# Means by VectorE's block transposes in two more groups, and Newton steps on GpSimd for every reciprocal root

## The chip, the cores and the metric

The kernel runs on one NeuronCore of a Trainium2 chip. The metric is the time of the device for one execution, in microseconds (us). The engines are TensorE (PE, its weight loads PEld), VectorE (DVE), ScalarE (ACT), GpSimd (POOL) and SyncE (SP), which starts nearly all of the DMAs.

## The reference

The first half is a linear attention with a norm over the 64 elements of a head; the second is a wide layer with the gate h * erf(softplus(h)). All in f32.

```
kv  = einsum('bhsd,bhse->bhde', k, v)          # b=8, h=8, s=576, d=64
out = einsum('bhsd,bhde->bhse', q, kv)
rms = sqrt(mean(out*out, axis=-1) + 1e-6)
x   = (out / rms * g_norm)                     # as 4608 rows of 512
h   = x @ w_in                                 # 512 -> 2048
g   = h * erf(softplus(h))
y   = g @ w_out                                # 2048 -> 512
```

## The kernel before

The 4608 rows are worked off in nine groups, T = 0 to 8, of 512 rows each: the first 512 of the 576 rows of each batch entry, and, as the last group, the eight remainders of 64 rows, which are collected in `x_last`. Within a group two heads together make 128 partitions, so a group has four pairs of heads p = 0 to 3, and x is held transposed, a block of 128 features (two heads) by 512 rows per pair. The mean over a head's 64 features is therefore a sum over 64 partitions.

The matrix products of the layer run over 16 units f of 128 hidden features, four units to a batch (`BATCH`). From group 1 on, h = x @ w_in is made of three fp32r products from two parts of each factor ("high" and "low" and a scaled sum, `upper`, `lower`, `product`), 12 matmuls of 128x512 for a block, into two PSUM banks n_ps and m_ps; three such pairs of banks go round (`pair_of_banks`). Group 0 uses plain f32 matmuls (L1201), and groups 0 and 1 use plain f32 for the second product (`project`, L834), with a lag of five units.

The work falls into four parts.

1. A prologue for group 0, in the order that `ORDER` writes out (`first_group`).
2. Groups 0 and 1 in the loop at L1156, a unit at a time. While group T is worked on, the attention of group T + 1 is made in pieces, which `pieces_of` (L1028) hands out to steps of the loop: for a pair, `visit` (the products with kv, into the PSUM tile `at`, and the square on ScalarE), then one step later `halve` and `keep_tail`, `mean`, in the step after that `norm` and the transpose of the next q (`turn`, L347), then `split`. Within a step the order of the code is: weights that are due (L1162: three or four VectorE instructions L281, L284, L287, L292 that join the two halves of the f64 words of w_in or w_out to f32), pieces of list 3 (L1166), parts of the weights (L1168), pieces of list 0 (L1170), more weights that are due (L1172), gates (L1082), the matmuls of h, the copy of h, softplus, pieces of list 1, the products of `project`, pieces of list 2. Each engine takes its instructions in this order. The weights are joined only during group 0.
3. The change to the third part (`held_sums`, L1110), with the last `mean`, `norm` and `split`.
4. Groups 2 to 8, in batches of four units (L1323), with all of their products in fp32r and all parts of the weights read back from DRAM. Here the attention of the next group is made for two pairs at once by `paired` (L542), at numbered places of a batch: place i + 1 after unit i, place 5 + j after the result of rows j.

In part 2 the mean is a matmul with a 128x128 matrix of 1/64 (`mean_w`); so that fp32r is exact enough, `halve` (L455) cuts the squares into two parts on VectorE (L459, L460) and `mean` (L462) makes four matmuls of 128x256 (L470, L471). The first pair of group 1 uses two plain f32 products instead (L476). The reciprocal root is then taken on ScalarE over 128x512: a logarithm (L482), an exponential of -0.5 times it (L483) and its square (L484), with two loads of activation tables around them (L114, L117), and `norm` adds one Newton step with two VectorE instructions (L490, L493) ahead of the product with `out` and `gm_col` (-0.5 g, L502).

In `paired`, VectorE transposes the squares in blocks of 32x32 (L629) and sums each block along the free axis (L630), so that 128x16 sums stand for 128x512 squares; four ScalarE copies of 32 partitions (L643) and an addition (L644) join the two blocks of a head. The root is taken on 128x32 for two pairs, also with logarithm, exponential and square (L649 to L651) and one Newton step (L658, L661), and a transpose of a broadcast (L665) spreads it back over 128x512, ahead of the product L674.

Of the kernel before, what the change touches and what calls it, by code (L numbers as in the profile page):

```python
# [39 lines left out]
FP32 = mybir.dt.float32  # L40
# [8 lines left out]
EPS = 1e-6  # L49
# [9 lines left out]
SQ = 32  # L59
BLOCKS = 16  # L60
ORDER = """
kv0 fill0 q0 fill1 q_out0 kv_out0 result0 kv1 kv_out1 q1 square0 q_out1 mean0 log0 result1 kv2 kv_out2
# [8 lines left out]
def kernel(  # L71
# [328 lines left out]
    def keep_prepared():  # L400
        kept.pop()()
        turn(1, 0)

    def attention(T, p):

        st = {}

        halves = T > 1 or (T == 1 and p > 0)
# [4 lines left out]
        two = halves_of  # L413

        bd = kv_of(T, p)

        def square_tile(name):
            return qt_tile(name)[:, 0:G]

        def visit():  # L420


            qT = ready.pop((T, p))
            at = st["at"] = at_tile()
            x = halves_of(qT[:, 0:G])
            for a, i in ((0, 0), (0, 1), (1, 0), (1, 1)):
                nc.tensor.matmul(  # L427
                    at[rows_of[i if a else 1 - i], a, 0 : 2 * P],
                    lhsT=bd[rows_of[i], a * D : (a + 1) * D],
                    rhs=x[rows_of[i], a],  # L430
                    start=True,
                    stop=True,
                )
# [11 lines left out]
            nc.scalar.activation(two(st["sq"]), st["o"], AF.Square)  # L445

# [7 lines left out]

        def halve():  # L455
            sq = st.pop("sq")
            hi = st["hi"] = attp.tile([P, G], FP32R, name="sq_hi", tag="rms_r")
            lo = st["lo"] = attp.tile([P, G], FP32R, name="sq_lo", tag="sq_lo")
            nc.vector.tensor_copy(out=hi, in_=sq)  # L459
            nc.vector.tensor_tensor(out=lo, in0=sq, in1=hi.bitcast(FP32), op=ALU.subtract)  # L460

        def mean(table=True):  # L462
            ms = st["ms"] = st["at"][:, :, 2 * P : 4 * P]
            parts = [(ms[:, a], a) for a in range(2)]
            if halves:


                hi, lo = two(st.pop("hi")), two(st.pop("lo"))
                for ps, a in parts:
                    nc.tensor.matmul(ps, lhsT=mean_w, rhs=hi[:, a], start=True, stop=False)  # L470
                    nc.tensor.matmul(ps, lhsT=mean_w, rhs=lo[:, a], start=False, stop=True)  # L471
                u = square_tile("u")
            else:
                u = st.pop("sq")
                for ps, a in parts:
                    nc.tensor.matmul(  # L476
                        ps, lhsT=mean_w.bitcast(FP32), rhs=two(u)[:, a], start=True, stop=True
                    )
            r = attp.tile([P, G], FP32, name="rms_r", tag="rms_r")
            exp_ln_table()  # L480
            st["u"], st["r"] = u, r
            nc.scalar.activation(two(r), ms, AF.Ln, bias=eps_col)  # L482
            nc.scalar.activation(r, r, AF.Exp, scale=-0.5)  # L483
            nc.scalar.activation(u, r, AF.Square)  # L484
            if table:
                softplus_table()

        def norm():
            ms, u, r = (st.pop(name) for name in ("ms", "u", "r"))
            nc.vector.scalar_tensor_tensor(  # L490
                out=two(u), in0=ms, scalar=EPS, in1=two(u), op0=ALU.add, op1=ALU.mult
            )
            nc.vector.scalar_tensor_tensor(  # L493
                out=u, in0=u, scalar=3.0, in1=r, op0=ALU.subtract, op1=ALU.mult
            )
            if T < FIRST:
# [3 lines left out]
            else:  # L500
                x = st["x"] = x_new.tile([P, G], FP32, name="x", tag="x")
            nc.vector.scalar_tensor_tensor(  # L502
                out=two(x),
                in0=st.pop("o"),
                scalar=gm_col,
                in1=two(u),
                op0=ALU.mult,
# [27 lines left out]
        then_ = partial(turn, *then)  # L535
        pieces = (first_, (visit, loads), (halve, keep_tail) if halves else (keep_tail,))
        return (*(partial(chain, *group) for group in pieces), mean, partial(chain, norm, then_), split)

# [3 lines left out]
    def paired(T, p):  # L542
# [75 lines left out]

        def small(name):
            t = twice[name] = attp.tile([P, 2 * BLOCKS], FP32, name=name, tag=name)  # L620
            return t

        def block_sums():


            total = small("ms")
            for n in range(2):
                t = attp.tile([P, G], FP32, name="sq_t", tag=("rms_r", "sq_lo")[n])
                nc.vector.transpose(out=t, in_=twice["x"][n])  # L629
                nc.vector.tensor_reduce(  # L630
                    out=total[:, n * BLOCKS : n * BLOCKS + BLOCKS],
                    in_=t.rearrange("p (c d) -> p c d", c=BLOCKS),
                    axis=AX.X,
                    op=ALU.add,
                )

        def across():


            total, other = twice["ms"], small("ms_other")  # L640
            for n in range(4):
                rows, beside = (slice(32 * k, 32 * k + 32) for k in (n, n ^ 1))
                nc.scalar.copy(other[rows], total[beside])  # L643
            nc.vector.tensor_tensor(out=total, in0=total, in1=other, op=ALU.add)  # L644

        def root():
            total, r, u = twice["ms"], small("rms"), small("rms_u")
            exp_ln_table()
            nc.scalar.activation(r, total, AF.Ln, bias=eps_col)  # L649
            nc.scalar.activation(r, r, AF.Exp, scale=-0.5)  # L650
            nc.scalar.activation(u, r, AF.Square)  # L651
            softplus_table()

        def spread():


            total, r, u = (twice[name] for name in ("ms", "rms", "rms_u"))
            nc.vector.scalar_tensor_tensor(  # L658
                out=u, in0=total, scalar=EPS, in1=u, op0=ALU.add, op1=ALU.mult
            )  # L660
            nc.vector.scalar_tensor_tensor(  # L661
                out=u, in0=u, scalar=3.0, in1=r, op0=ALU.subtract, op1=ALU.mult
            )
            for n in range(2):
                nc.vector.transpose(  # L665
                    out=twice["x"][n].rearrange("p (c d) -> p c d", c=BLOCKS),
                    in_=u[:, n * BLOCKS : n * BLOCKS + BLOCKS].unsqueeze(2).to_broadcast([P, BLOCKS, 32]),
                )

        def norm(n):  # L670
            x = twice["x"][n]
            if T < B:
                x = halves_of(x)
            nc.vector.scalar_tensor_tensor(  # L674
                out=x, in0=twice["o", n], scalar=gm_col, in1=x, op0=ALU.mult, op1=ALU.mult
            )
# [21 lines left out]
        if side == 0:  # L698
            first = {0: (q_loads,), 2: (visit, square, keep, kv_loads)} if T < B else {0: (square,)}
            norms = [partial(norm, n) for n in range(2)]  # L700
            pieces = first | {3: (block_sums,), 4: (across,), 5: (root,), 6: (spread,), 8: norms}
        else:
# [325 lines left out]
    def pieces_of(T):  # L1028
# [3 lines left out]
        for p in range(NP):  # L1032
            products, apply, halve, mean, norm, split = attention(T, p)
            f = (BATCH - 1) * (p + 1) if T < FIRST else BATCH * p
# [4 lines left out]
            else:  # L1039
                steps[f + 1][1].append(apply)  # L1040
            steps[f + 2][3].append(halve)
            with_erf = (f + 2) % BATCH == BATCH - 1

            place = 2 if T < FIRST and p == 0 else 1
            if T == FIRST and p == NP - 1:
                ending.extend((partial(mean, table=False), norm, split))
                continue
            steps[f + 2][place].append(partial(mean, table=not with_erf))
            steps[f + 3][0].append(norm)
# [60 lines left out]
    def held_sums():  # L1110

        mean, norm, split = ending
        mean()
        units = range(whole - BATCH, whole)
# [208 lines left out]
    for m in range(first_batch, batches + 1):  # L1323
# [60 lines left out]
        if m < batches:  # L1384
            for i in range(1 if last_ else 2):
                nc.scalar.activation(part(s, i), part(s, i), AF.Erf)  # L1386
            if not last_ and (b % 2 or not todo):
                softplus_table()
# [63 lines left out]
```

## Time and profile before

| | us |
|---|---|
| median of 3 runs (884.7 to 885.28) | 885.0 |
| the profiled execution | 885.01 |
| its span, first to last instruction | 883.2 |
| granted TensorE clock, mean | 1.000 |

The page has a table of each engine's busy time, its share of the span and its instructions, and then the span in 40 slices of 22.1 us with the busy share in tenths (9 is 90% or more). TensorE's matmuls are pipelined and the ends of their records are modelled: a matmul of 128x512 is recorded with 0.39 us but the next starts 0.227 us later in fp32r and 0.429 us later in plain f32, so the starts are what to read.

In the views in order of time a line has: start, duration, engine, line of the code, operation, the tile written <- the tiles read, shapes, how many instructions were merged, and in brackets the idle time of the engine before it with what ended it. L1082, L740 and so on are lines of the code above; a helper has one line for all of its callers, and the tiles tell them apart.

The parts of the kernel lie in the trace like this: the prologue up to some 22 us, the loop of group 0 up to 128 us, that of group 1 up to 222 us, the change to the batches up to some 236 us, then 14 pairs of batches of about 46 us each.

### The profile page before, as it was taken

What the parts mean: (1) busy time and instruction counts of PE and PEld (TensorE: products, weight loads), DVE (VectorE), ACT (ScalarE), POOL (GpSimd) and SP (SyncE); (2) the same over time, 40 slices, a digit from 0 to 9 for tenths busy, and PEclk for the clock granted to TensorE, in tenths of its full rate; (3) what the DMA queues carried; (4) which work ended last, traced back from release to release, by engine and by line L of the source; (5) the groups of instructions that cost most, each with busy time, mean ns of one, the idle gap of its engine ahead of it and who ended that gap; (6) DMA issues with size and microseconds to landing.
All of it is one profiled execution on the core that took longest, in us unless ns stands there. A gap on an engine that the chain in (4) does not pass through costs nothing.

```text
span 883.2 us, 13286 instructions
## 1 busy us (share of the span) xinstructions
PE 875.1 (99%) x4874; PEld 659.1 (75%) x4874; DVE 752.6 (85%) x1107; ACT 559.3 (63%) x789; POOL 4.7 (1%) x14
## 2 busy tenths in 40 slices
PE   8999999999999999999999999999999999999998
PEld 4444456666788888888888888888888888888887
DVE  5889978899998898989898989898979797966667
ACT  5977677777775657565665647474757575755552
POOL 2000000000000000000000000000000000000000
PEclk9999999999999999999999999999999999999999
DMA  9977427989799997999799979998797779778871
GB/s 291 291 225 224 132 75 285 342 310 341 262 358 401 330 347 251 385 328 349 232 382 350 353 231 346 366 342 295 272 351 282 288 288 344 289 279 334 316 255 49
DMA packets 136929, 259.89 MB, mean 294 GB/s; under 512 B 78816, under 2 KB 87264, under 8 KB 136864
## 3 DMA queue, kind: packets, MB, share of 16 engines
q1 hardware_dynamic: 136128, 258.09, 82.8%
q10 hardware_dynamic: 544, 0.82, 0.3%
q8 instruction: 39, 0.64, 0.3%
q14 instruction: 26, 0.21, 0.1%
q0 software_dynamic: 192, 0.13, 0.0%
HBM read 224.40 MB, written 34.60 MB: 293 GB/s over the span
## 4 chain that ended last, share of the span: by engine, by line
PE 91%; DMA 3%; DVE 2%; ACT 2%; issue 1%; SPq 0%; DVEq 0%; ACTq 0%
PE n_ps L778 48%; PE m_ps L778 24%; PE o_ps L834 8%; PE h_ps L1201 5%; DMA w_out_parts<-w_out 1%; PE at_ps L557 1%; DMA q_sb<-in_q_dram 1%; PE off_ps L588 1%; DMA w_in<-w_new 1%; PE warm_ps L982 1%; DMA w_in_parts<-w_in 0%; PE at_ps L427 0%; ACT s_sb L1154 0%; PE at_ps L440 0%; ACT L1154 0%
## 5 line engine op out<-in xcount | busy, mean ns | idle before, releaser
L778 PE MATMUL n_ps<-w_out_parts,g_forms 128*128 128x512 f32 (+1 forms) x936 | 230.1, 388 | 0.2 <-DMA w_out_parts<-w_out 0.2
L778 PE MATMUL n_ps<-x_forms,w_in_parts 128*128 128x512 f32 x896 | 222.6, 390 | 0.0
L778 PEld LDWEIGHTS n_ps<-w_out_parts,g_forms 128*128 128x128 f32 x936 | 175.0, 188 | 36.7 <-DMA w_out_parts<-w_out 0.9
L778 PEld LDWEIGHTS n_ps<-x_forms,w_in_parts 128*128 128x128 f32 x896 | 167.4, 188 | 35.1
L753 DVE TENSOR_TENSOR h<-m_ps,h 128x512 f32<-128x512 f32 x116 | 78.5, 686 | 58.6 <-PE m_ps L778 58.5
L1358 ACT ACTIVATE h<-n_ps 128x512 f32<-128x512 f32 x112 | 66.7, 596 | 94.0 <-PE n_ps L778 91.8
L1363 ACT ACTIVATE s<-h 128x512 f32<-128x512 f32 x112 | 69.2, 632 | 88.6 <-DVE h L753 88.6
L778 PE MATMUL m_ps<-w_out_parts,g_forms 128*128 128x512 f32 x464 | 123.9, 389 | 0.0
L778 PE MATMUL m_ps<-x_forms,w_in_parts 128*128 128x512 f32 x448 | 119.7, 389 | 0.0
L778 PEld LDWEIGHTS m_ps<-w_out_parts,g_forms 128*128 128x128 f32 x464 | 87.1, 188 | 18.1
L778 PEld LDWEIGHTS m_ps<-x_forms,w_in_parts 128*128 128x128 f32 x448 | 84.1, 188 | 17.5
L753 DVE TENSOR_TENSOR e<-m_ps,e 128x512 f32<-128x512 f32 x116 | 80.1, 692 | 14.1 <-PE m_ps L778 3.4
L834 PE MATMUL o_ps<-w_out_sb,h_sb 128*128 128x512 f32 x192 | 86.8, 595 | 0.0
L713 ACT ACTIVATE g_forms<-h 128x1024 fp32r<-128x1024 f32 x58 | 60.8, 1061 | 39.2 <-PE m_ps L778 21.0
L719 DVE SCALAR_TENSOR_TENSOR g_forms<-g_forms 128x1024 fp32r<-128x1024 f32 x58 | 71.1, 1226 | 2.0
L716 DVE TENSOR_TENSOR g_forms<-h,g_forms 128x1024 fp32r<-128x1024 f32 x58 | 70.5, 1215 | 0.5 <-ACT g_forms L713 0.4
L1412 DVE TENSOR_TENSOR h<-h,s 128x1024 f32<-128x1024 f32 x56 | 65.9, 1217 | 0.0
L834 PEld LDWEIGHTS o_ps<-w_out_sb,h_sb 128*128 128x128 f32 x192 | 35.5, 190 | 38.3 <-issue 36.9
L748 DVE SCALAR_TENSOR_TENSOR e<-n_ps,e 128x512 f32<-128x512 f32 (+1 forms) x89 | 59.8, 671 | 3.4 <-PE n_ps L778 3.4
L1201 PE MATMUL h_ps<-xT,w_in_sb 128*128 128x512 f32 x128 | 57.9, 596 | 1.3 <-DVE w_in_sb L292 1.2
L117 ACT ACT_TABLE_LOAD x43 | 55.2, 1283 | 0.8
L1386 ACT ACTIVATE s<-s 128x1024 f32<-128x1024 f32 x50 | 50.6, 1054 | 0.3
(166 smaller groups left out, 936.6 us busy)
## 6 DMA issues: line engine op xcount, KB each, us to landing
w_out_parts<-w_out SPq DMA_DIRECT2D x116, 768.0 KB, 7.2
w_in_parts<-w_in SPq DMA_DIRECT2D x112, 768.0 KB, 6.7
w_in<-w_new SPq DMA_DIRECT2D x16, 768.0 KB, 4.8
k_sb<-in_k_dram SPq DMA_DIRECT2D x32, 288.0 KB, 6.1
v_sb<-in_v_dram SPq DMA_DIRECT2D x31, 288.0 KB, 5.7
w_raw<-in_moe_w_in_dram SPq DMA_DIRECT2D x16, 512.0 KB, 6.3
w_raw<-in_moe_w_out_dram SPq DMA_DIRECT2D x8, 1024.0 KB, 5.3
out_dram<-e SPq DMA_DIRECT2D x32, 256.0 KB, 4.0
```

The source lines that it names most:

```text
L117: nc.scalar.preload_act_table_set("softplus")
L713: nc.scalar.activation(high, x, AF.Copy, scale=1.0 + 2.0**-13)
L716: nc.vector.tensor_tensor(out=low, in0=x, in1=high.bitcast(FP32), op=ALU.subtract)
L719: nc.vector.scalar_tensor_tensor(out=both, in0=low.bitcast(FP32), scalar=SHIFT, in1=high.bitcast(FP32), op0=ALU.mult, op1=ALU.add,)
L748: nc.vector.scalar_tensor_tensor(out=out_, in0=ps, scalar=scale, in1=out_, op0=ALU.mult, op1=ALU.add)
L753: nc.vector.tensor_tensor(out=out_, in0=ps, in1=out_, op=ALU.add)
L778: nc.tensor.matmul(ps[:, cols], lhsT=weights(form, k), rhs=moving(form, k)[:, cols], start=(form == forms[0] and k == 0), stop=(form == fo ...
L834: nc.tensor.matmul(o_ps[j], lhsT=g[:, j * P : j * P + P], rhs=one(w_out_sb, f), start=(f == 0), stop=last,)
L1201: nc.tensor.matmul(plain[i], lhsT=blocks_of(one(w_in_sb, i % FC))[:, c], rhs=xT[T][:, c, :], start=(c == 0), stop=(c == KC - 1),)
L1358: nc.scalar.activation(h[:, i], n_ps, AF.Copy, scale=SHIFT - 1.0)
L1363: nc.scalar.activation(s[:, i], h[:, i], AF.Softplus)
L1412: nc.vector.tensor_tensor(out=part(h, half), in0=part(h, half), in1=part(s, half), op=ALU.mult)
```

## The change

`attention`, which serves groups 1 and 2, gets the way of `paired`: the squares are transposed and summed by VectorE, and `halve`, the matmuls of `mean` and the wide logarithm, exponential and square go. And every root, in both, is taken on GpSimd: the addition of the two blocks, of epsilon, a first guess from the bits of the float, and three Newton steps, 15 instructions on 128x16 or 128x32. The table load for softplus after each batch's erf, which the root's own load had covered in every other batch, now stands there always.

```diff
+NEWTON = 3
+    def sums_of_blocks(squares):
+        total = small("ms", len(squares))
+        for n, x in enumerate(squares):
+            t = attp.tile([P, G], FP32, name="sq_t", tag=("rms_r", "sq_lo")[n])
+            nc.vector.transpose(out=t, in_=x)
+            nc.vector.tensor_reduce(
+                out=total[:, n * BLOCKS : n * BLOCKS + BLOCKS],
+                in_=t.rearrange("p (c d) -> p c d", c=BLOCKS),
+                axis=AX.X,
+                op=ALU.add,
+            )
+        return total
+    def roots(total):
+        n = total.shape[1] // BLOCKS
+        other, m, y, a = (small(name, n) for name in ("ms_other", "ms_eps", "rms", "rms_a"))
+        for k in range(4):
+            rows, beside = (slice(32 * i, 32 * i + 32) for i in (k, k ^ 1))
+            nc.scalar.copy(other[rows], total[beside])
+        two, one_ = nc.gpsimd.tensor_tensor, nc.gpsimd.tensor_scalar
+        two(out=m, in0=total, in1=other, op=ALU.add)
+        one_(out=m, in0=m, scalar1=EPS, scalar2=None, op0=ALU.add)
+        one_(
+            out=y.bitcast(I32),
+            in0=m.bitcast(I32),
+            scalar1=-0.5,
+            scalar2=float(0x5F3759DF),
+            op0=ALU.mult,
+            op1=ALU.add,
+        )
+        for _ in range(NEWTON):
+            two(out=a, in0=y, in1=y, op=ALU.mult)
+            two(out=a, in0=a, in1=m, op=ALU.mult)
+            one_(out=a, in0=a, scalar1=-0.5, scalar2=1.5, op0=ALU.mult, op1=ALU.add)
+            two(out=y, in0=y, in1=a, op=ALU.mult)
+        return y
+    def spread_over(xs, y):
+        for n, x in enumerate(xs):
+            nc.vector.transpose(
+                out=x.rearrange("p (c d) -> p c d", c=BLOCKS),
+                in_=y[:, n * BLOCKS : n * BLOCKS + BLOCKS].unsqueeze(2).to_broadcast([P, BLOCKS, 32]),
+            )
...
-        def halve():
...
-        def mean(table=True):
...
+        def block_sums():
+            st["ms"] = sums_of_blocks([st["sq"]])
+        def root():
+            st["r"] = roots(st["ms"])
         def norm():
...
+            u = st.pop("sq")
+            spread_over([u], st.pop("r"))
...
-        pieces = (first_, (visit, loads), (halve, keep_tail) if halves else (keep_tail,))
+        pieces = (first_, (visit, loads), (keep_tail, block_sums), (root,), (norm, then_), (split,))
...
-            pieces = first | {3: (block_sums,), 4: (across,), 5: (root,), 6: (spread,), 8: norms}
+            pieces = first | {3: (block_sums,), 4: (root,), 6: (spread,), 8: norms}
...
-            steps[f + 2][3].append(halve)
-            steps[f + 2][place].append(partial(mean, table=not with_erf))
+            steps[f + 2][3].append(keep)
+            steps[f + 2][0].append(root)
...
-            if not last_ and (b % 2 or not todo):
+            if not last_:
                 softplus_table()
```

So in a step of part 2 the sums stand where `halve` stood (list 3), the root stands in list 0 of the same step, and the spread at the beginning of `norm`, in list 0 of the next step. In `paired` the sums stay at place 3, the root begins at place 4 instead of 5, and the spread stays at place 6. The square that feeds the sums is scaled by 1/64 on the way (0.125 inside the square), and `norm` multiplies by g instead of -0.5 g. `first_group` is not changed.

More of the change, by code (lines that the diff above doesn't have):

```diff
@@ L402, in keep_prepared, with small @@
         turn(1, 0)
+    def small(name, n):
+        return attp.tile([P, 2 * BLOCKS], FP32, name=name, tag=name)[:, 0 : n * BLOCKS]
+    def sums_of_blocks(squares):
[39 more added lines that the diff above has]
+            )
     def attention(T, p):
         st = {}
-        halves = T > 1 or (T == 1 and p > 0)
         then = divmod(T * NP + p + 1, NP)
@@ L411, in attention @@
         more_cols = slice(kv_cols.stop, kv_cols.stop + D)
-        two = halves_of
         bd = kv_of(T, p)
-        def square_tile(name):
-            return qt_tile(name)[:, 0:G]
         def visit():
@@ L444, in visit @@
             st["sq"] = qT[:, 0:G]
-            nc.scalar.activation(two(st["sq"]), st["o"], AF.Square)
+            nc.scalar.activation(halves_of(st["sq"]), st["o"], AF.Square, scale=0.125)
         def keep_tail():
@@ L453, in keep_tail @@
                 kv_kept(then[0], 1, st["at"], more_cols)
-        def halve():
[L456 to L460, printed above, removed]
-        def mean(table=True):
[L463 to L486, printed above, removed]
-        def norm():
[L489 to L495, printed above, removed]
+        def block_sums():
+            st["ms"] = sums_of_blocks([st["sq"]])
+        def root():
+            st["r"] = roots(st["ms"])
+        def norm():
+            u = st.pop("sq")
+            spread_over([u], st.pop("r"))
             if T < FIRST:
@@ L502, in norm @@
             nc.vector.scalar_tensor_tensor(
-                out=two(x),
+                out=halves_of(x),
                 in0=st.pop("o"),
-                scalar=gm_col,
-                in1=two(u),
+                scalar=g_col,
+                in1=halves_of(u),
                 op0=ALU.mult,
@@ L535, in attention @@
         then_ = partial(turn, *then)
-        pieces = (first_, (visit, loads), (halve, keep_tail) if halves else (keep_tail,))
-        return (*(partial(chain, *group) for group in pieces), mean, partial(chain, norm, then_), split)
+        pieces = (first_, (visit, loads), (keep_tail, block_sums), (root,), (norm, then_), (split,))
+        return (partial(chain, *group) for group in pieces)
     twice = {}
@@ L617, in square @@
                 nc.scalar.activation(x, o, AF.Square, scale=0.125)
-        def small(name):
-            t = twice[name] = attp.tile([P, 2 * BLOCKS], FP32, name=name, tag=name)
-            return t
         def block_sums():
[L626 to L644, printed above, removed]
-        def root():
[L647 to L652, printed above, removed]
-        def spread():
[L657 to L668, printed above, removed]
+            twice["ms"] = sums_of_blocks(twice["x"])
+        def root():
+            twice["r"] = roots(twice["ms"])
+        def spread():
+            spread_over(twice["x"], twice["r"])
         def norm(n):
@@ L674, in norm @@
             nc.vector.scalar_tensor_tensor(
-                out=x, in0=twice["o", n], scalar=gm_col, in1=x, op0=ALU.mult, op1=ALU.mult
+                out=x, in0=twice["o", n], scalar=g_col, in1=x, op0=ALU.mult, op1=ALU.mult
             )
@@ L1032, in pieces_of @@
         for p in range(NP):
-            products, apply, halve, mean, norm, split = attention(T, p)
+            products, apply, keep, root, norm, split = attention(T, p)
             f = (BATCH - 1) * (p + 1) if T < FIRST else BATCH * p
@@ L1040, in pieces_of @@
                 steps[f + 1][1].append(apply)
-            steps[f + 2][3].append(halve)
-            with_erf = (f + 2) % BATCH == BATCH - 1
-            place = 2 if T < FIRST and p == 0 else 1
+            steps[f + 2][3].append(keep)
+            steps[f + 2][0].append(root)
             if T == FIRST and p == NP - 1:
-                ending.extend((partial(mean, table=False), norm, split))
+                ending.extend((norm, split))
                 continue
-            steps[f + 2][place].append(partial(mean, table=not with_erf))
             steps[f + 3][0].append(norm)
@@ L1110, in held_sums @@
     def held_sums():
-        mean, norm, split = ending
-        mean()
+        norm, split = ending
         units = range(whole - BATCH, whole)
```

## The prediction

> **What bounds the kernel now.** The profiled execution took 885.01 us, its span 883.2; the median of the three runs shown is 885.0, so sums on the profile go straight to the median. I read the busy table and the slices of the page first.
>
> ```profile
> PE 875.1 (99%) x4874; PEld 659.1 (75%) x4874; DVE 752.6 (85%) x1107; ACT 559.3 (63%) x789; POOL 4.7 (1%) x14
> PE   8999999999999999999999999999999999999998
> DVE  5889978899998898989898989898979797966667
> ```
>
> TensorE has hardly an idle moment, at a granted clock of 1.000. So only two things move the time: matmuls that go, and waits that make TensorE stop. VectorE is second, and full in slices 3 to 6 (65 to 130 us), the loop of group 0. It runs in program order there, and TensorE takes from it the joined weights (L292) and the gates (L1082). The third view is TensorE in order of time, around one mean of that loop:
>
> ```profile
> 65.99 3.60 PE L1201 MATMUL h_ps<-xT,w_in_sb 128*128 128x512 f32 x8
> 69.03 0.68 PE L470 MATMUL at_ps<-sq_hi,mean_w 128*128 128x256 f32 x1
> 69.55 0.28 PE L471 MATMUL at_ps<-sq_lo,mean_w 128*128 128x256 f32 x1
> 69.66 0.28 PE L470 MATMUL at_ps<-sq_hi,mean_w 128*128 128x256 f32 x1
> 69.78 0.28 PE L471 MATMUL at_ps<-sq_lo,mean_w 128*128 128x256 f32 x1
> 69.90 3.60 PE L834 MATMUL o_ps<-w_out_sb,h_sb 128*128 128x512 f32 x8
> ```
>
> Read the starts: four matmuls of a mean hold TensorE from 69.03 to 69.90, 0.87 us, most of it in the first (0.52 to the next start; it is the step from plain f32 to fp32r).
>
> **TensorE's part.** Three such means in the loop of group 0 give 3 x 0.87 = 2.6 us. In the loop of group 1 the neighbours are fp32r already and a mean costs 0.48 (141.68 to 142.16); three give 1.4. The fourth there (222.04) is followed by a matmul that waits for g_held until 222.90 anyway: nothing, at most 0.47. The plain-f32 mean of the first pair (49.26 to 50.12) also gives nothing, because the next matmul waits for a join:
>
> ```profile
> 49.26 1.03 PE L476 MATMUL at_ps<-qT,mean_w 128*128 128x256 f32 x4
> 50.78 3.70 PE L1201 MATMUL h_ps<-xT,w_in_sb 128*128 128x512 f32 x8 [0.50 <-DVE w_in_sb L292]
> ```
>
> So 4.0 us at the most. Twelve pairs of later groups (`paired`) have no matmul that goes.
>
> **ScalarE's part.** A root of a pair goes from 70.89 to 75.50: two table loads of 1.28 and three activations, 4.6 us, against four copies (0.89 for four at 388.93). ScalarE is 63% busy and mostly waits for TensorE (91.8 us for L1358 alone). Worth nothing here. The same holds for the table loads of `paired`.
>
> **VectorE's part, by rows.** Gone per pair: halve, 63.23 to 64.30, 1.07 (not in the first pair), and two of the three instructions of norm, 74.23 to 75.68, 1.45. Added: a transpose with a reduce, 1.34 (384.88 to 386.22 in `paired`), ahead of the next join, and one spreading transpose, 0.65. Net 0.53 less per pair, but 0.54 more in the first, of which 1.34 lies ahead of the join that TensorE waits for at 50.78. That join would end at 50.73 + 1.34 = 52.1: 1.3 us lost, whatever else happens.
>
> **GpSimd's part, not in this trace.** A root is 15 instructions on 128x16 or 128x32, each on the result of the last. The only rows:
>
> ```profile
> 0.72 0.20 POOL masks.py:197 MEMSET ident<- 128x128 f32 x1 [0.29 <-POOLq L1433]
> 1.00 0.29 POOL masks.py:199 TENSOR_SCALAR_AFFINE_SELECT ident<-ident 128x128 f32<-128x128 f32 x1
> 9.75 0.22 POOL L232 TENSOR_SCALAR gm_col<-g_col 128x1 f32<-128x1 f32 x1 [4.65 <-DMA g_col<-in_g_norm_dram]
> 1.91 0.39 DVE L213 CAST mean_w<-mean_f 128x128 fp32r<-128x128 f32 x1
> ```
>
> Lower end 0.10 each (memset of 128x1), upper 0.29 + 0.08 (the gap from 0.92 to 1.00 between two dependent ones): 1.5 to 5.6 us a chain. I take the nearest row, 0.22 + 0.08 = 0.30: 4.5 us. Is that hidden? For the second pair ScalarE is busy with erf and a table until 68.0, so its copies end at 68.9 and the chain at 73.4; the spread is wanted at 74.2. The other pairs have more room (first: copies done at 49.1, spread wanted at 56.5). Alone, the chain is just hidden.
>
> The open question is whether the two engines get in each other's way. The last row above is the one hint: this cast of 128x128 takes 0.39 while GpSimd starts DMAs (1.49 to 4.05), and L459, the same cast four times as wide, takes 0.42 with GpSimd at rest; by its width it should be near 0.2. Between root and spread stand eight or nine VectorE instructions (L281, L284, L287, L292, L1082, and the four again) with no gap:
>
> ```profile
> 65.37 0.68 DVE L281 TENSOR_SCALAR w_e<-w_raw 128x1024 f32<-128x1024 f32 x1
> 66.08 0.69 DVE L284 TENSOR_SCALAR w_e<-w_e 128x1024 int32<-128x1024 int32 x1
> ...
> 74.23 0.69 DVE L490 SCALAR_TENSOR_TENSOR u<-at_ps,u 128x512 f32<-128x512 f32 x1 [0.38 <-ACT u L484]
> ...
> 122.96 0.65 DVE L1082 TENSOR_TENSOR h_sb<-h_sb,s_sb 128x512 f32<-128x512 f32 x1
> ```
>
> If they exclude each other, one link of the chain fits between two of these, and the six or seven links left run while the spread, and all of VectorE behind it, waits. VectorE's loss per chain lies between 0 (hidden) and 4.5 (every link costs it its full time). I take 3.0: about 8 links that hold up VectorE for part of their time (8 x 0.12) and 7 in full (7 x 0.30).
>
> The Trainium skill has a rule on this, "SBUF — State Buffer", section "Who interferes with whom": a VectorE instruction with two SBUF inputs, or one in a two-port mode, and a GpSimd instruction that reads SBUF shut each other out, and whichever comes second waits for the other to finish. The cast above fits it, and by it nearly every instruction of that stretch collides; taken literally the loss is 3 to 4.5 us per chain, where the rows without the rule allow 0. It speaks against this change.
>
> **The sum.** VectorE in the loop of group 0, lateness after each pair: first +1.34 - 0.80 + 3.0 = 3.5. Second: -0.53 - 0.38 (the old wait) + 3.0, total 5.6. Third: -0.53 + 3.0, less the 0.52 of idle time at 102.6, total 7.6. Fourth: -0.53 + 3.0, less 0.71 and 1.10 of idle time (116.3 and 120.2), total 8.3. The last gate of the loop ended at 122.96 + 0.65 = 123.61 and ends at 131.9. TensorE uses it in the second half of this row,
>
> ```profile
> 121.64 7.03 PE L834 MATMUL o_ps<-w_out_sb,h_sb 128*128 128x512 f32 x16
> ```
>
> at 121.81 + 3.43 = 125.24; it starts 6.7 later, the means that went included, as TensorE waits anyway. In the loop of group 1 VectorE idles some 10 us in 90 and the bank that it frees has 3.3 us to spare (add over at 177.27, bank written again at 180.55): 2.5 per chain is absorbed, and the three means give 1.4. Sum: 885.0 + 6.7 - 1.4 = 890.3.
>
> `paired` adds nothing by this price. Copies are over at 389.82; L719 (two SBUF inputs) runs to 390.63; then four VectorE instructions read PSUM, until 393.44; two long products h*s follow, then the spread:
>
> ```profile
> 393.44 2.35 DVE L1412 TENSOR_TENSOR h<-h,s 128x1024 f32<-128x1024 f32 x2
> 395.70 0.18 DVE L658 SCALAR_TENSOR_TENSOR rms_u<-ms,rms_u 128x32 f32<-128x32 f32 x1
> 396.15 1.30 DVE L665 STREAM_TRANSPOSE x<-rms_u 128x512 f32<-128x512 f32 x2
> 397.38 0.65 DVE L748 SCALAR_TENSOR_TENSOR e<-n_ps,e 128x512 f32<-128x512 f32 x1
> ...
> 400.32 1.98 PE L778 MATMUL n_ps<-x_forms,w_in_parts 128*128 128x512 f32 x8
> ```
>
> Nine links fit ahead of 393.4, two between the products, four after: spread at 397.0, 0.9 late. The bank that L748 frees at 398.03 is written again at 400.32, three products on: 2.3 us to spare, which hides it.
>
> **Rivals.**
> 1. *The chain stays hidden* (0 in place of 3.0). For: 4.5 us fits each gap, and no row shows GpSimd slowing a tensor_tensor. Against: the cast, and VectorE's full slices. Only the late join remains, 1.3 lost, and 2.6 + 1.4 of means won: 885.0 - 2.7 = 882.3, faster. With a loss of S per chain the sum above is 4S - 6.7; it falls below this rival's -2.7 at S = 1.0, so this decides up to there.
> 2. *A link costs 0.40 or more.* For: 0.37 is within the rows; a two-input form isn't among them. The loss per chain is 4.0 or more, so 4 x 4.0 - 6.7 = 9.3; in `paired` the spread comes at 398.6, 2.45 late, 0.15 over what is spare, twelve times: 2. Together 885.0 + 11.3 = 896; at 0.50 a wait of 1.6 in each pair makes it over 910.
> 3. *Half of it*: with S from 1.2 to 2.1 the loss cancels against the means: 883.2 to 886.8.
>
> **Chances.** Forecast (886.8 to 896) 0.45, rival 1 0.24, rival 3 0.14, rival 2 0.17. A measurement can tell about 0.2% (1.8 us) from no change. Faster 0.24, same 0.14, slower 0.45 + 0.17 = 0.62. Range 882 to 898: it reaches rival 1's 882.3 and the beginning of rival 2, and leaves out about 0.1 on each side. Since both signs are in it: the forecast's own range is 886.8 to 896.
>
> **What would show it.** POOL with 20 x 15 = 300 more instructions, links near 0.3 us where VectorE reads PSUM and longer starts between them elsewhere. VectorE idle ahead of the spread, released by POOL, 1.5 us and more per pair in the loop of group 0; L281 and L292 longer there than 0.68 and 1.23. TensorE waiting for gates near 85, 107 and 125, and for the join at 50.8 until about 52.5. No such wait in `paired`. I am wrong if VectorE doesn't wait for POOL, or if the waits lie in `paired`.

## The result, and the profile after

The changed kernel takes 895.98 us (median of 4 runs, 894.73 to 896.73) against 885.02 (884.7 to 885.28): a ratio of 1.0123, with a 95% interval of 1.0105 to 1.0140. That is 11.0 us slower. The profiled execution took 896.19 us, its span is 894.4 and the mean granted clock 0.995. One execution below, the profiled one of run 3 (1105.41 us at a granted clock of 0.751), is left out of every comparison.

The busy table and TensorE's slices, as in the first fence of the prediction:

```profile
PE 877.7 (98%) x4842; PEld 657.0 (73%) x4842; DVE 744.7 (83%) x1065; ACT 505.6 (57%) x735; POOL 133.7 (15%) x314
PE   8989999999899999999999999999999999999998
```

POOL has 300 instructions more, VectorE 42 and ScalarE 54 fewer; 32 matmuls have gone. TensorE has new pauses in slices 3 and 11 (of 22.4 us each). The view of waits names them; the columns are total us, number of waits and the longest:

```profile
PE o_ps L808 <- DVE h_sb L1053: 3.6, 2, 1.9
PE h_ps L1171 <- DVE w_in_sb L293: 3.5, 2, 2.8
PE n_ps L752 <- ACT h L1186: 2.7, 1, 2.7
```

Before, of these three, only the second was there, with 1.2 us. But waits of 9.8 us, 8.6 more than before, in a kernel with 32 matmuls fewer, don't make 11.0. For an account I set the start of the same matmul in both traces side by side:

| TensorE starts | before | after | later by |
|---|---|---|---|
| h_ps behind the first join | 50.78 | 52.18 | 1.40 |
| first product of group 1's loop | 128.11 | 133.74 | 5.63 |
| near the end of that loop | 216.40 | 220.34 | 3.94 |
| n_ps behind the copy of h | 219.26 | 226.15 | 6.89 |
| m_ps of the same unit | 221.11 | 229.11 | 8.00 |
| first batch of group 2 | 250.53 | 257.15 | 6.62 |
| end of group 2 | 329.31 | 336.47 | 7.16 |
| beginning of group 5 | 513.04 | 521.48 | 8.44 |
| last batch | 875.36 | 886.45 | 11.09 |

So there are three losses: 5.6 in the loop of group 0, 4.1 near 222 us, and 4.5 that grow slowly from 250 us to the end, where hardly a wait is to be seen (0.3 for a DMA near 278). Group 1's loop and the change to the batches give 3.1 back (1.69 and 1.38): 5.6 + 4.1 + 4.5 - 3.1 = 11.1. The first is the one that was forecast.

**The loop of group 0.** These rows of the timeline answer to the prediction's rows around 50.78 and 121.64; the idle time ahead of a row stands in brackets:

```profile
52.18 5.37 PE L1171 MATMUL h_ps<-xT,w_in_sb 128*128 128x512 f32 x8 [2.81 <-DVE w_in_sb L293]
...
111.39 3.70 PE L808 MATMUL o_ps<-w_out_sb,h_sb 128*128 128x512 f32 x8 [1.86 <-DVE h_sb L1053]
...
130.60 3.70 PE L808 MATMUL o_ps<-w_out_sb,h_sb 128*128 128x512 f32 x8 [1.78 <-DVE h_sb L1053]
```

The join ends at 52.03 (52.1 was forecast), but the eight matmuls behind it take 5.37 in place of 3.70: in this trace the granted clock is 0.5 from 52.81 to 56.22. In the view of stretches it is the third number from the end:

```profile
52.81:56.22 3.41, 3.41 (x6) 1.35 (x5) 3.21 (x4) 0.42 (x1) 3.16 (x4) 0.50 1.01 357
226.89:230.30 3.41, 3.41 (x9) 2.65 (x9) 3.16 (x5) 2.23 (x4) 3.00 (x6) 0.50 1.09 351
```

Behind that VectorE's gates come late, and TensorE waits for them in the other two rows. The reason for it is in the timeline of VectorE and GpSimd; here is one of the four chains of this loop:

```profile
95.36 1.22 DVE L288 SCALAR_TENSOR_TENSOR w_e<-w_raw,w_e 128x1024 int32<-128x1024 int32 x1
95.49 1.21 POOL L433 TENSOR_SCALAR ms_eps<-ms_eps 128x16 f32<-128x16 f32 x1
96.61 1.23 DVE L293 CUSTOM_DVE_ANT_0 w_out_sb<-w_e,w_m 128x2048 uint16<-128x2048 uint16 x1
96.78 1.13 POOL L434 TENSOR_SCALAR rms<-ms_eps 128x16 int32<-128x16 int32 x1
...
102.58 0.22 POOL L444 TENSOR_TENSOR rms_a<-rms_a,ms_eps 128x16 f32<-128x16 f32 x1
102.89 0.20 POOL L445 TENSOR_SCALAR rms_a<-rms_a 128x16 f32<-128x16 f32 x1
...
104.63 0.71 DVE L453 STREAM_TRANSPOSE qT<-rms 128x512 f32<-128x512 f32 x1 [2.21 <-POOL rms L446]
```

L433 and L434 are links like L444 and L445, on 16 elements a partition; but while one of these VectorE instructions runs beside them they last until 0.1 us after its end, 1.2 in place of 0.2. One link is done per VectorE instruction. When VectorE comes to the spread, seven links are left (ten in the second chain), and they take 7 x 0.30 = 2.1 while it waits. VectorE's own instructions have the durations of before (1.23 and 1.23, 0.68 for L282; the longest of L288 is 1.24 in both traces): in this trace it is not the one that is held up.

**Near 222 us.** The timeline of ScalarE, VectorE and TensorE there:

```profile
223.86 0.69 DVE L415 TENSOR_REDUCE ms<-sq_t 128x16 f32<-128x512 f32 x1
224.63 0.84 ACT L430 COPY ms_other<-ms 32x16 f32<-32x16 f32 x4 [2.53 <-DVE ms L415]
225.50 0.60 ACT L1186 ACTIVATE h<-n_ps 128x512 f32<-128x512 f32 x1
226.15 0.51 PE L752 MATMUL n_ps<-x_high,w_new 128*128 128x512 f32 x1 [2.73 <-ACT h L1186]
```

The four small copies of the last pair of group 2 stand in ScalarE's order ahead of the copy of h. They wait 2.53 for VectorE's sums, and so does the copy of h, whose bank TensorE wants. Again the granted clock is 0.5 behind the pause, from 226.89 to 230.30 (the second row of stretches above).

**From 250 us on.** In `paired` the spread is 0.8 late against TensorE (405.04; 396.15 + 8.09 would be 404.24), and no wait of TensorE follows:

```profile
405.04 1.30 DVE L453 STREAM_TRANSPOSE x<-rms 128x512 f32<-128x512 f32 x2 [1.44 <-POOL rms L446]
406.27 0.65 DVE L722 SCALAR_TENSOR_TENSOR e<-n_ps,e 128x512 f32<-128x512 f32 x1
...
408.41 2.02 PE L752 MATMUL n_ps<-x_forms,w_in_parts 128*128 128x512 f32 x8
```

But compare the last row with its counterpart at 400.32 in the prediction: 2.02 for eight matmuls in place of 1.98. From one start to the next (the pitch, averaged over a group, pauses left out), the products of x_forms with w_in_parts take about 232.6 ns in groups 3, 5 and 7 and about 227 in groups 2, 4, 6 and 8; before it was about 227 in all of them. The products with w_out_parts stay at 227. The granted clock is 1.0 throughout. A group has 16 units of 12 such matmuls, 192 x 5.8 ns = 1.1 us; with the tenths of a nanosecond of the other products it is 1.2 of the 1.3 us that the table gives for group 3 (7.16 late at 329.31, before it, and 8.44 at 513.04, behind groups 3 and 4). Groups 5 and 7 with what follows them add 2.65, as much for each.

### The profile page after: what moved, and what is told of

Same layout as the page of the kernel before. It is cut to its first block, busy times and chain, and to the rows that moved or that the text cites. A ratio compares the mean times of both kernels' runs of the same rounds, so it can differ in the third digit from the quotient of the medians.

```text
span 894.4 us, 13441 instructions
## 1 busy us (share of the span) xinstructions
PE 877.7 (98%) x4842; PEld 657.0 (73%) x4842; DVE 744.7 (83%) x1065; ACT 505.6 (57%) x735; POOL 133.7 (15%) x314
## 4 chain that ended last, share of the span: by engine, by line
PE 84%; DVE 6%; DMA 3%; POOL 3%; ACT 2%; issue 1%; SPq 0%; DVEq 0%; ACTq 0%
PE n_ps L752 48%; PE m_ps L752 24%; PE o_ps L808 5%; PE h_ps L1171 2%; DMA w_out_parts<-w_out 2%; DMA w_in_parts<-w_in 1%; PE at_ps L573 1%; DVE w_e L288 1%; PE off_ps L604 1%; POOL rms_a L443 1%; PE warm_ps L956 1%; DVE w_e L285 0%; POOL rms_a L444 0%; PE o_ps L1069 0%; ACT s_sb L1124 0%
## 5 line engine op out<-in xcount | busy, mean ns | idle before, releaser
L727 DVE TENSOR_TENSOR h<-m_ps,h 128x512 f32<-128x512 f32 x116 | 78.5, 686 | 54.4 <-PE m_ps L752 52.8
L432 POOL TENSOR_TENSOR ms_eps<-ms,ms_other 128x32 f32<-128x32 f32 (+1 forms) x20 | 13.4, 670 | 607.4 <-ACT ms_other L430 607.4
L727 DVE TENSOR_TENSOR e<-m_ps,e 128x512 f32<-128x512 f32 x116 | 80.3, 692 | 13.2 <-PE m_ps L752 2.3
L722 DVE SCALAR_TENSOR_TENSOR e<-n_ps,e 128x512 f32<-128x512 f32 (+1 forms) x89 | 59.8, 672 | 3.3 <-PE n_ps L752 3.3
```

Source lines behind the costliest of these rows:

```text
L722: nc.vector.scalar_tensor_tensor(out=out_, in0=ps, scalar=scale, in1=out_, op0=ALU.mult, op1=ALU.add)
L727: nc.vector.tensor_tensor(out=out_, in0=ps, in1=out_, op=ALU.add)
```

## The experiments

Theory one: there are three separate losses (VectorE's wait for the chain, ScalarE's copies in front of the copy of h, and something in the later groups that isn't a wait). Its rivals: that the loss is one cause, GpSimd beside VectorE, all the way to the end; and that VectorE is late by its own added instructions.

**1. The new means with the new roots in groups 1 and 2 alone.** `paired` keeps logarithms, and the tiles for them.

```diff
...
-            pieces = first | {3: (block_sums,), 4: (root,), 6: (spread,), 8: norms}
+            pieces = first | {3: (block_sums,), 4: (across,), 5: (root,), 6: (spread,), 8: norms}
...
```

> The changed kernel, but `paired` takes its roots by logarithm on ScalarE as before; only groups 1 and 2 use GpSimd (8 chains). Theory: the loss up to 250 us of the trace (the matmuls there start 7.1 us later than before) belongs to groups 1 and 2, so it stays: about 892. If the further 4 us that build up between 257 and 884 us come from GpSimd at work in `paired`, they go and the time is 892; if they come from something that the early waits set off, they stay and it is 896. Rival, the loss is in `paired`: about 885 or less.

Measured: 891.35 us against 885.39, ratio 1.0066 (1.0051 to 1.0081). TensorE is 6.71 late at 250.53, as in the full change, and 6.51 at 875.36: nothing is lost from there on, and the pitch is about 227 ns in all groups.

**2. The new roots in `paired` alone.** `attention` is that of before.

> The kernel before, but `paired` takes its roots by Newton steps on GpSimd (12 chains); groups 1 and 2 keep matmul means and logarithms. Theory: the 1.4 us that VectorE waits ahead of each spread are inside the 2.3 us that the bank has to spare, so nothing: 885.0. If GpSimd's work itself slows TensorE's matmuls between 257 and 884 us, 889. Rival, a wait of TensorE in each pair: over 889.

Measured: 888.41 us, ratio 1.0037 (1.0025 to 1.0050). TensorE is 0.12 early at 250.53, and 3.74 late at 875.36, with no wait of its own for the chain and the pitch of about 232.6 ns in groups 3, 5 and 7. So the chain in `paired` is hidden from TensorE, as forecast, and yet this half of the change costs 3.9 us between these two marks of its trace (3.0 by the medians).

**3. Means by transposes, every root by logarithms on ScalarE.** No work on GpSimd.

```diff
-        two(out=m, in0=total, in1=other, op=ALU.add)
...
+        nc.vector.tensor_tensor(out=total, in0=total, in1=other, op=ALU.add)
+        exp_ln_table()
+        nc.scalar.activation(r, total, AF.Ln, bias=eps_col)
+        nc.scalar.activation(r, r, AF.Exp, scale=-0.5)
+        nc.scalar.activation(u, r, AF.Square)
+        softplus_table()
...
```

> Only the first half of the change: means of groups 1 and 2 by VectorE's transposes, every root by logarithm, exponential and square on ScalarE over the small sums, with one Newton step on VectorE; no GpSimd. Theory: the two waits for gates (1.9 and 1.9 us, at 109 and 128 us) go with the chain, while the late join (1.4 us and as much again of half clock after it) and ScalarE's copies in front of the copy of h at 224 us (2.9 us and then half clock, 1.6) stay: 896 - 3.9 = 892, and 888 if the slow drift goes too. Rival, that GpSimd isn't what costs: 895 to 896.

Measured: 901.33 us, ratio 1.0178 (1.0161 to 1.0195). That is above both of the expected times, and slower than the change itself. Run 12 below takes it up.

**4. The Newton steps on VectorE.** One line of the changed kernel.

```diff
-        two, one_ = nc.gpsimd.tensor_tensor, nc.gpsimd.tensor_scalar
+        two, one_ = nc.vector.tensor_tensor, nc.vector.tensor_scalar
```

> The changed kernel with the 15 instructions of each root on VectorE in place of GpSimd. At the 0.18 to 0.19 us of its instructions on 128x32 and 0.03 between them a chain is 3.2 us of VectorE's time, against a wait of 2.2 to 3.1 us in group 0 now. Theory (only the wait counts, VectorE loses no time to GpSimd otherwise): about the same in the loop of group 0, 1 to 3 us worse there; in `paired` 3.2 - 0.5 late against 2.3 to spare, 0.4 us in each of twelve pairs, 5 in all: 897 to 904. If GpSimd and VectorE slowed each other beyond that wait: below 896.

Measured: 918.67 us, ratio 1.0379 (1.0364 to 1.0395), worse than expected. A link costs VectorE 0.21 us:

```profile
103.18 0.17 DVE L432 TENSOR_TENSOR ms_eps<-ms,ms_other 128x16 f32<-128x16 f32 x1 [0.91 <-ACT ms_other L430]
103.39 0.17 DVE L433 TENSOR_SCALAR ms_eps<-ms_eps 128x16 f32<-128x16 f32 x1
```

Fifteen of them are 3.1, and VectorE's wait for ScalarE's copies, which with the chain on GpSimd it doesn't have, comes on top: 0.91 here. TensorE is 17.4 late at 128.11, where the change on GpSimd has 5.63. The run also shows the slow pitch (about 233 ns) in groups 3, 5 and 7, with no instruction of the chain on GpSimd: GpSimd is not its cause. What it shares with the change is a fifth small tile in the pool attp, 128 bytes per partition, and the pools that are opened behind attp on the left side, w_in_parts among them, are moved by it.

**5. The copies behind the copy of h.** One piece moved: the root of the last pair of group 2.

```diff
-            steps[f + 2][0].append(root)
+            steps[f + 2][1 if T == FIRST and p == NP - 1 else 0].append(root)
```

> The changed kernel with one piece moved: the root of the last pair of group 2 (its four ScalarE copies and its chain on GpSimd) stands in list 1 of its step, behind ScalarE's copy of h, in place of list 0, ahead of it. Theory A (the copies stand in ScalarE's order ahead of the copy of h, wait 2.5 us there for VectorE's sums, and TensorE waits 2.7 us for that copy and then runs its plain f32 matmuls at half pace for 3.4 us): that wait near 222 us goes, 2.9 of wait and 1.1 to 1.6 of half clock, 3.2 to 4.5 us in all; 891.5 to 892.8 us in place of 896.0. Theory B (TensorE would wait there for VectorE's later results anyway, since VectorE is late): less than 1 us won, 895 to 896, with the wait moved to a result of VectorE.

Measured: 892.62 us (891.96 to 893.23) against 885.35, ratio 1.0081 (1.0069 to 1.0093): 3.4 won of the change's 11.0. Theory A holds. The same place in its timeline:

```profile
221.77 0.60 ACT L1186 ACTIVATE h<-n_ps 128x512 f32<-128x512 f32 x1 [0.42 <-PE n_ps L752]
222.50 0.42 PE L752 MATMUL n_ps<-x_high,w_new 128*128 128x512 f32 x1
...
225.08 0.84 ACT L430 COPY ms_other<-ms 32x16 f32<-32x16 f32 x4
```

The copy of h no longer waits for VectorE, TensorE goes on at once, and the four copies come 3.3 us behind it.

**6. The tiles of before's size.** The sum in place, four small tiles in attp for five.

```diff
-        other, m, y, a = (small(name, n) for name in ("ms_other", "ms_eps", "rms", "rms_a"))
+        m = total
+        other, y, a = (small(name, n) for name in ("ms_other", "rms", "rms_a"))
```

> The changed kernel with the sum, and the addition of epsilon to it, written in place: four small tiles in the pool attp in place of five, so that attp is 128 bytes per partition smaller, as large as before the change; the instructions are the same otherwise. Theory A (the slow matmuls of the groups 3, 5 and 7 come from where the tiles lie: every pool behind attp is moved by 128 bytes): the pitch of the matmuls of x_forms with w_in_parts in these groups goes from 232.6 back to 226.7 ns, and 3.9 us are won, 892 us. Theory B (they come from GpSimd's chains or from VectorE's other instructions beside them): pitch and time stay, 895.5 to 896.5.

Measured: 891.35 us, ratio 1.0065 (1.0052 to 1.0077), 4.6 won. TensorE is 6.50 late at 250.53 and 6.29 at 875.36; the pitch is about 227 ns everywhere. Theory A holds.

**7. The kernel before with 128 unused bytes.**

```diff
+    attp.tile([P, 2 * BLOCKS], FP32, name="unused", tag="unused")
```

> The kernel before with nothing added but a tile of 128 bytes per partition in the pool attp that nothing writes or reads. Theory A (places): the pitch of the matmuls of x_forms with w_in_parts in the groups 3, 5 and 7 rises from 226.7 to 232.6 ns and the time by 3.5 to 4 us, to 888.5 to 889; nothing else in the trace moves. Theory B (GpSimd's chains or VectorE's instructions): no difference, 885.0 within 0.5.

Measured: 888.85 us, ratio 1.0037 (1.0025 to 1.0050): 3.5 us for a tile that nothing touches, and the pitch in groups 3, 5 and 7 is about 232.6 ns. The row of group 3 in its timeline that answers to 400.32 (1.98) before, line L778 being L779 there:

```profile
400.46 2.02 PE L779 MATMUL n_ps<-x_forms,w_in_parts 128*128 128x512 f32 x8
```

**8. All that is late, moved, with two Newton steps.** Run 5's and run 6's edits; first sums and root of group 1's first pair in list 1; norm in list 1.

```diff
-NEWTON = 3
+NEWTON = 2
...
-            steps[f + 3][0].append(norm)
+            steps[f + 3][1].append(norm)
```

> The changed kernel with all that its trace shows as late taken up: the sums and the root of group 1's first pair stand in list 1 of their step, behind the gate and the matmuls' weights, the root of the last pair of group 2 in list 1 (as in the run that moves only that), the spread and norm of every pair of groups 1 and 2 in list 1 of their step in place of list 0; the sum is written in place (four small tiles); and two Newton steps in place of three, so 11 links for 15, which leaves the last step of the refinement out. Theory A (each of the losses has its own place: VectorE's wait for a chain 2.4 us a pair in the loop of group 0, the first join, the copy of h at 222 us, the tiles' places): all of the 11 us goes and part of the means that went is left over, 882 to 885 us. Theory B (VectorE's lateness in the loop of group 0 is in its own added instructions and in the later norm, which now holds up the transposes of q and the visits): 887 to 891.

Measured: 882.92 us (882.07 to 884.16, 10 runs), ratio 0.9974 (0.9965 to 0.9982): 2.4 us faster than the kernel before, though it leaves the third Newton step out, so that its roots are less exact. TensorE is 0.80 early at 128.11 and 2.22 at 216.40, and VectorE's waits for POOL ahead of the spread fall from 13.6 to 3.6 us.

**9. Run 5's and run 6's edits together.**

> The changed kernel with the two repairs of the earlier runs together: the sum in place (four small tiles in attp) and the root of the last pair of group 2 in list 1 of its step. Theory A (the two losses are separate): both gains add up, 3.4 and 4.6 us as measured alone, 888 us (887.5 to 888.7), and what is left over the kernel before, 2.5 to 3.5 us, is the loop of group 0 alone, less the means that went. Theory B (they overlap): 889.5 or more.

Measured: 888.67 us, ratio 1.0045 (1.0031 to 1.0059). The gains add up (7.3 together, 3.4 + 4.6 alone, each known to about 1.2), so the two losses are separate. What remains, 3.6, is the loop of group 0 (TensorE 4.74 late at 128.11) less the means in the loop of group 1 (1.46).

**10. The same with seven links.** Two of the three Newton steps are left out, so that the roots are less exact.

```diff
-NEWTON = 3
+NEWTON = 1
```

> The same two repairs, and one Newton step in place of three: a chain of 7 links for 15 (the last two steps of the refinement are left out, so that the roots are less exact). Theory A (what is late in the loop of group 0 is VectorE's wait for the chain, 2.2 to 3.1 us a pair): 8 links fewer end the chain at least 2.4 us earlier (8 x 0.30), the wait ahead of the spread goes to under 0.7 us, TensorE no longer waits for gates near 107 and 125, and 3 to 5 us are won: 883 to 885. Theory B (VectorE is late by the sums, which stand ahead of the join, and by the pause at 49 us with half the clock behind it): at most 1 us won, 887 to 888.5.

Measured: 884.05 us, ratio 0.9990 (0.9981 to 0.9999): 4.6 us for eight links in each chain. The wait ahead of the spread is gone in all pairs but one (0.71), and with it TensorE's waits for the gates: it starts the products of `project` that stood at 111.39, and at 110.51 in run 9, at 108.11,

```profile
98.59 0.70 DVE L454 STREAM_TRANSPOSE qT<-rms 128x512 f32<-128x512 f32 x1
...
108.11 3.70 PE L809 MATMUL o_ps<-w_out_sb,h_sb 128*128 128x512 f32 x8
```

with no wait in brackets. The late join is still there (h_ps 1.74 late), and at 128.11 only 0.30 is left: the three means that went gave 1.44, 0.48 each. Theory A holds: in this loop the price is the wait for the chain.

**11. Run 8 with all three Newton steps.**

> The kernel with the moved pieces (first pair's sums and root behind the gate, root of the last pair behind the copy of h, spread and norm in list 1 of their step, sum in place), with all three Newton steps, so that nothing of the computation is left out. Theory A (the moves hide the chain): within 0.7 us of the run with two steps, 882.3 to 883.7, VectorE's wait for POOL ahead of the spread in group 0 under 1.5 us a pair. Theory B (the shorter chain made the difference): four links of 0.3 to 1.2 us more a pair are waited for, 885 to 887.

Measured: 885.58 us, ratio 1.0007 (0.9998 to 1.0016). That is what theory B gave: of run 8's gain, 2.7 us by the two medians come from the shorter chain, and the moves hide the whole chain only in part. Ahead of the spread VectorE still waits 8.6 us for GpSimd, 3.4 of it in the first pair, where run 8 had 3.6 in all. The transpose of the next q now stands behind the late spread, and TensorE's visit waits for it:

```profile
63.54 0.66 PE L476 MATMUL at_ps<-qT,bd_kv 64*64 64x256 f32 x8 [1.52 <-DVE qT L348]
```

Three such waits make 3.1 us. With nothing left out, the best version is as fast as the kernel before.

**12. Run 3 with run 5's edit.**

> The kernel that has the means by transposes but every root by logarithms on ScalarE, with the root of the last pair of group 2 in list 1 of its step in place of list 0. Theory A (there too the copies, and with them two table loads and three activations, stand ahead of the copy of h that TensorE waits for near 222 us): 4 to 6 us won against the 901.3 without the move, 895.5 to 897.5. Theory B (its loss lies in the loop of group 0, where VectorE's addition waits for ScalarE's copies): stays at 900 to 901.5.

Measured: 896.72 us, ratio 1.0134 (1.0120 to 1.0148), 4.6 less than run 3: theory A. For the rest of its loss the trace has VectorE waiting for ScalarE; these are waits of VectorE between 20 and 240 us:

```profile
DVE h_sb L744 <- ACT h_sb L1203: 8.3, 3, 2.8
DVE ms L429 <- ACT ms_other L428: 6.8, 5, 3.1
```

VectorE's addition of the two blocks waits for four small copies in ScalarE's order, with all of VectorE behind it. With the addition on GpSimd, as in run 9 (888.67), VectorE doesn't have that wait, but 14.6 us of waits for the chain ahead of the spread. TensorE is 7.02 late at 128.11 here, 4.74 there. No run takes these waits of run 12 away one at a time, so what each of them costs is not shown; another 3.7 us are lost between 216.41 and 250.53.

**13 to 15. What about the place counts.** In both kernels stand two tiles on the right side, `shift` and `shift_r`, that no instruction writes or reads. Run 13 is the changed kernel and run 14 the kernel before, both with

```diff
-... .tile([P, 496], FP32, name="shift_r")
+... .tile([P, 464], FP32, name="shift_r")
```

and run 15 is run 7 with 256 bytes in place of 128.

> The changed kernel with the unused tile shift_r on the right side 128 bytes per partition smaller (464 words for 496), so that late_r, gate_r and w_out_p move by 128 bytes too. Theory A (the distance between w_in_parts on the left and x_forms on the right counts): the pitch in the groups 3, 5 and 7 is 226.7 ns again, and the time 891 to 892.5 us, as with the smaller attp. Theory B (the place of the left pools itself counts): pitch 232.6 ns, 895.5 to 896.5 us.

> The kernel before with shift_r 128 bytes per partition smaller and nothing else. Theory A (the distance counts): the slow pitch of 232.6 ns appears in the groups 3, 5 and 7, 888.5 to 889 us, as with the unused tile on the left. Theory B (the left pools' own place counts): no difference, 885.0 within 0.5.

> The kernel before with an unused tile of 256 bytes per partition in attp in place of the 128 of the earlier run. The run with the new means in groups 1 and 2 alone had 256 bytes more there and kept 226.7 ns. Theory A (the effect repeats every 256 bytes): no loss, 885.0 within 0.5, pitch 226.7 ns everywhere. Theory B (any move off the tuned place costs): 888.5 or more, pitch above 230 ns in the groups 3, 5 and 7.

Measured: run 13 892.14 us, ratio 1.0076 (1.0062 to 1.0089), pitch about 227 ns; run 14 889.90, 1.0047 (1.0035 to 1.0060), a little more than expected, pitch about 232.6 in groups 3, 5 and 7; run 15 884.83, 0.9996 (0.9988 to 1.0005), pitch about 227. Theory A each time. What counts is the distance between the tiles on the left and those on the right: moving both by 128 bytes is as good as moving neither, and a move by 256 of one does no harm. Among the products of groups 2 to 8 those that slow down are w_in_parts, on the left, with x_forms of the odd groups, on the right; those whose two operands lie on one side do not. The products of group 1's loop with w_new take some 231 to 236 ns in every trace at the full clock, the kernel before among them, so they are no part of the difference; what slows them is not shown.

## Why the prediction failed

The direction and the place of the forecast loss were right, and the sum was half of what came: +5.3 forecast, +11.0 measured. Two things that the sum has at nothing, ScalarE's part and the places of the tiles, cost more together than all that it has. By its steps:

- *"... four matmuls of a mean hold TensorE from 69.03 to 69.90, 0.87 us ..."* Mis-sized: 0.48. The record of the first starts before the last matmul of h_ps is through; eight of those take 8 x 0.429 = 3.43 from 65.99, so the mean begins at 69.42. Three means gave 1.44 in run 10, not 2.6. The forecast's own sum doesn't use this term, rival 1's does. In the loop of group 1, 1.4 was forecast and 1.35 to 1.7 measured.
- *"That join would end at ... 52.1: 1.3 us lost."* Right: 1.40. Missed was the half clock behind the pause, 1.67 on the eight matmuls; TensorE's next wait for a gate, 1.86 at 111.39, is longer than that and covers it.
- *"I take the nearest row, 0.22 + 0.08 = 0.30."* Right: links at rest last 0.20 to 0.23 on 128x16, 0.30 from start to start.
- *"I take 3.0: about 8 links that hold up VectorE for part of their time (8 x 0.12) and 7 in full (7 x 0.30)."* The second half is what was measured, 2.2, 3.1, 2.2 and 2.2 us in the loop of group 0; the first is nothing. The row of the cast that took 0.39 led me to a VectorE that is slowed; here GpSimd alone is held up. Four chains made 9.7 us of waits, not 12, the last gate of the loop came 6.9 late (122.96 to 129.90), not 8.3, and TensorE 5.5, not 6.7: the matmuls that wait for it started at 125.08 in the trace before (121.64 + 8 x 0.43; the prediction's 125.24 is 0.16 too late) and at 130.60 after.
- *"`paired` adds nothing by this price"* and *"0.9 late"*: right, 0.8, and no wait of TensorE in runs 2 and 9.
- *"ScalarE is 63% busy and mostly waits for TensorE ... Worth nothing here."* This is the first step that failed. I weighed its busy time and not its order: the root was moved to list 0, ahead of the copy of h, and I named nothing that was queued behind its wait. Near 222 us that cost 2.95 of wait and 1.11 of half clock; run 5 won 3.4.
- *Not in the prediction at all*: where the tiles lie. This is the second step that failed, since the sum has the matmuls of the later groups at their old pitch. The diff adds a tile to a pool, and the kernel has two unused tiles by the name of shift, which suggest that the place was chosen. Price 3.5 (run 7) to 4.6 (run 6).

With these two terms the forecast's 890.3 becomes 890.3 + 3.4 + 3.5 to 4.6 = 897.2 to 898.3; less what the chain was priced too dear (1.2, the 6.7 against 5.5) it is 896.0 to 897.1, and 895.98 was measured. That it lies at the very end of the forecast's range, 886.8 to 896, is luck: more than half of the loss comes from what the sum doesn't have. Rival 2 named nearly this time (896) for another reason, a link of 0.40 or more and waits in `paired`: a free link goes from start to start in 0.30, and no TensorE wait stands in `paired`.

## What to carry to other kernels

When a piece moves in a static order, look at what stands behind it on each engine that it uses, the idle ones too: four copies, 0.84 us together, on an engine that was 57% busy cost more than 3 us (run 5), because they waited ahead of a copy that TensorE needed. A diff that adds or drops a tile moves all that is allocated behind it; where two builds differ with no wait to show for it, compare the pitch of the same matmuls and try an unused tile of the difference. A long chain of small instructions on GpSimd beside a full VectorE went forward here by one link per VectorE instruction that reads SBUF alone; count the links that are left when VectorE needs the result. Eight links fewer gave 4.6 us (run 10).

## What the runs showed of the hardware

**GpSimd gives way.** In the changed kernel's trace a link of 0.22 us lasts 0.40 to 1.29 beside L282, L285, L288, L293 and L1053, and 0.21 to 0.29 beside L722 and L727, which read PSUM. The Trainium skill, "SBUF — State Buffer", section "Who interferes with whom", has an exclusive lock on a pair of SBUF ports that VectorE and GpSimd share, which whoever issues first keeps for its whole instruction. The rows agree with the lock; of the two orders they show only one. In the chain shown above VectorE's next instruction starts 0.03 us after the last one's end, and GpSimd's next link 0.08 us after its own last one, later each time.

**Half the clock after a pause.** The clock goes to 0.5 for exactly 3.413 us after some of TensorE's pauses: at 52.81 and 226.89 in the changed kernel, 174.08 apart, 51.0 times 3.413, so the spells start on a grid of that width (runs 1, 6 and 13 have two spells each, also 174.08 apart). Measured from start to start less a matmul's own pitch, pauses of 2.97 and 2.90 us were followed by one there, and 2.47 in run 5; pauses of 2.07 and 1.94 in the changed kernel, and 2.96 and 2.97 in runs 5 and 10, were not. In run 4 the spells last 6.827, with pauses of 6.97 and 4.19. The Trainium skill, "TensorE: Matmul & The Clock Gate", section "What's actually happening", has a free-running window of 3413 ns, with half the clock after an idle window. The grid agrees; but here a pause well short of a window is enough in some runs. Each spell takes up to 3.413 / 2 = 1.7 us.

**The pitch of a matmul can depend on where its two operands lie.** In groups 3, 5 and 7 it is about 227 or 232.6 ns for the same shapes, by a change of 128 bytes in the distance between the two sides (runs 6, 7, 13 to 15), with the granted clock at 1.0 in both. Which part of the chip this comes from is not shown.
